# Transposed tiles by DMA in a two-layer transformer kernel: tokens and attention output leave TensorE and ScalarE

## The chip, the cores and the metric

One core of a Trainium2 chip runs the whole program. A core has five engines that each follow their own list of instructions in order: PE (TensorE, matrix products into the PSUM banks, with weight loads shown apart as PEld), DVE (VectorE), ACT (ScalarE), POOL (GpSimd, which has no access to PSUM) and SP (SyncE, which here only issues DMAs). They meet at semaphores. The metric is the device time of one execution in microseconds (us), the median of several.

## The reference

Two equal layers act on 2048 tokens of width 512. Each layer is an attention block with 32 heads of width 16 and a feed-forward block (FFN) of width 1792, both behind a layer norm and with a residual sum. Both layers use the same weights.

```python
x = A_x
x = x + _A_ref(_layernorm(x, axis=-1), A_wqkv, A_wo)
x = x + _B_ref(_layernorm(x, axis=-1), B_w_gate, B_w_up, B_w_down)
x = x + _A_ref(_layernorm(x, axis=-1), A_wqkv, A_wo)
x = x + _B_ref(_layernorm(x, axis=-1), B_w_gate, B_w_up, B_w_down)

# _A_ref: scores = q @ k.T * Dh ** -0.5; softmax over the keys; times v; heads joined; @ wo
# _B_ref: (gelu(x @ w_gate) * (x @ w_up)) @ w_down
```

## The kernel before

**Tiles.** X holds the tokens in float32, 16 tiles of 128 tokens on the partitions. A matrix product contracts over partitions, so each consumer needs its input transposed: XNT holds the normalised tokens with the model dimension on the partitions (four chunks of 128), ATTT the same for 128 tokens of attention output. KT holds the transposed keys, eight head groups (g, four heads each) by 2048 keys in four blocks of 512 (kb); a head has 32 rows there, 16 of keys and others that carry a bias of -1, so that the row maximum written beside the query is subtracted inside the product. QT holds up to eight units of queries in the same form.

**Two passes over the scores.** A unit is a block of 128 to 512 queries times one head group; there are 80. The first pass (line 1711) makes the scores with queries on the partitions and DVE takes the row maxima (line 1726, one or two banks at a time). The maxima are joined on POOL (lines 1071 to 1073), transposed in small blocks by DVE into MT, and SP moves them into QT (line 1115). The second pass (line 1581) makes the transposed scores with the maxima subtracted, ACT takes exponentials into SCR (line 1557), and PE multiplies them with the values (line 1605) into bank 7. A "fold" shifts work between the engines: PE makes the product of the queries with the difference of two key blocks (KD, line 1530), ACT takes its relu (line 1537), and DVE needs one combined step (line 1721) in place of the two blocks' maxima. `want_fold` decides by how far the first pass leads the second.

**The planner.** The order of every engine's instructions is written out when the program is built. Generators ("chains") yield what they need next: an engine with the tiles read and written, or a condition. The main loop of `_build` keeps an estimated clock for each engine, steps chains for DVE, POOL and ACT as soon as their operands are estimated ready, SP chains when the operands are due within 0.5 us and SP's clock within 0.8, and picks for PE between first pass, second pass and the rest by due times. Every DMA issue is estimated at 0.63 us of SP (`T_DMA`), and its end at 1.6 us later plus a given duration. When PE would stand still, the planner puts in products with a tile of zeros (line 1750). Every 16 steps of the first pass the next row of PLAN sets 21 constants, among them the lead at which copies go to DVE (LAGT), the thresholds for fillers, for folds and for how much other work PE takes between the passes.

**Where the tiles are transposed.** `ln_to_xnt` (line 874) normalises up to four tiles, by POOL alone (`ln_pool`), by DVE and POOL (`ln_head`), or in the head and the very last block by faster forms; the normalised tile goes to one of two buffers XN. Then `transpose_tile` (line 847) takes a bank, makes four PE transposes (line 855) and copies the bank to XNT with `evac`, on ACT (line 709) or DVE (line 707) by `pick`. Tags name the place: ("in", layer) ahead of the attention, ("mid", layer) ahead of the FFN. `outproj` does the same with ATT and two buffers ATTT, ahead of the product with WO. `ffn` takes a lock (`gel["on"]`) after its tiles are transposed in the plan; while it is held the second pass has no exponentials, since ACT has another function table loaded. In the head, six copies on ACT and two on POOL (line 564, `kt_fill`) fill KT with the bias rows before keys are moved in by SP (line 928).

```python
            if rd:
                for e, i in rd.items():
                    need((e, i))
```

These lines, in `_Sched.op`, turn a reader of a tile into a dependency of its next writer. A DMA group is a semaphore; a serial group counts its transfers one after another.

Of the kernel before, what the change touches and what calls it, by code (L numbers as in the profile page):

```python
# [21 lines left out]
    (0.2, 0.1, 0.55, 0.42, 0.3, -0.05, 1, 0, 30, 76, 8, 20, 0.3, 2.0, 0, 6, 1, 2, 9, 1, 0.0),  # L22
    (0.2, 0.1, 0.55, 0.42, 0.3, -0.05, 1, 0, 30, 76, 8, 20, 0.3, 2.0, 0, 6, 1, 2, 9, 1, 0.0),
    (0.1, 0.35, 0.65, 0.52, 0.2, -0.05, 1, 1, 102, 84, 13, 60, -0.1, 2.0, 0, 2, 1, 4, 5, 1, 0.0),
    (0.1, 0.15, 0.55, 0.32, 0.2, -0.05, 2, 1, 70, 84, -12, 40, 0.3, 2.0, 10, 2, 2, 2, 6, 1, 0.0),
    (0.3, 0.1, 0.55, 0.0, 0.0, -0.05, 2, 0, 14, 84, 8, 40, 0.3, 1.0, 0, 2, 2, 2, 5, 2, 0.0),
    (0.2, 0.1, 0.55, 0.42, 0.3, -0.05, 2, 0, 30, 84, 8, 60, 0.3, 2.0, -5, 2, 4, 3, 7, 1, -0.05),
    (0.2, 0.1, 0.65, 0.62, 0.3, -0.05, 1, 2, 30, 84, 8, 60, 0.3, 1.5, -5, 2, 4, 3, 9, 4, -0.05),
    (0.2, 0.1, 0.55, 0.62, 0.3, -0.05, 1, 2, 30, 84, 8, 60, 0.3, 2.0, -5, 2, 4, 3, 9, 1, -0.05),
    (0.2, 0.1, 0.55, 0.62, 0.3, -0.15, 1, 2, 30, 84, 8, 60, 0.3, 2.0, -5, 2, 4, 3, 9, 1, -0.05),  # L30
    (0.2, 0.1, 0.55, 0.62, 0.3, -0.15, 1, 2, 30, 84, 8, 50, 0.3, 2.0, -5, 2, 4, 2, 9, 1, -0.05),
    (0.2, 0.1, 0.55, 0.62, 0.3, -0.05, 1, 2, 30, 84, 8, 60, 0.3, 2.0, -5, 2, 4, 3, 9, 1, -0.05),
    (0.2, 0.1, 0.55, 0.62, 0.3, -0.1, 1, 2, 30, 116, 8, 60, 0.3, 2.0, -5, 2, 1, 3, 9, 1, -0.05),
    (0.4, 0.1, 0.65, 0.42, 0.3, -0.05, 3, 0, 5, 84, 8, 60, 0.3, 3.5, 20, 6, 2, 3, 3, 1, 0.2),
    (0.35, 0.15, 0.65, 0.12, 0.3, -0.05, 3, 0, 5, 84, 8, 60, 0.3, 1.0, 15, -6, 2, 3, 3, 1, 0.05),
    (0.2, 0.05, 0.55, 0.42, 0.3, -0.05, 2, 0, 30, 84, 8, 60, 0.3, 2.0, -5, 2, 4, 3, 7, 1, -0.05),
    (0.2, 0.05, 0.55, 0.42, 0.3, -0.05, 2, 0, 30, 84, 8, 60, 0.3, 2.0, -5, 2, 4, 3, 7, 1, -0.05),
    (0.2, 0.1, 0.55, 0.62, 0.3, -0.05, 1, 2, 30, 84, 8, 60, 0.3, 2.0, -5, 2, 4, 3, 9, 4, -0.05),
    (0.2, 0.1, 0.55, 0.52, 0.3, 0.0, 2, 0, 30, 84, 8, 60, 0.3, 2.0, -5, 2, 4, 3, 7, 1, -0.05),
    (0.15, 0.1, 0.55, 0.42, 0.0, -0.05, 3, 0, 70, 76, -2, 80, 0.7, 2.0, 15, 2, 2, 1, 7, 3, 0.2),  # L40
    (0.15, 0.1, 0.55, 0.32, 0.0, -0.05, 3, 0, 70, 76, -2, 80, 0.7, 2.0, 10, 2, 2, 1, 3, 3, 0.2),
    (0.3, 0.15, 0.55, 0.42, 0.2, 0.0, 2, 0, 38, 84, 8, 40, 0.3, 2.0, 0, -14, 2, 2, 5, 2, 0.0),
    (0.3, 0.15, 0.55, 0.42, 0.2, 0.0, 2, 0, 38, 84, 8, 40, 0.3, 2.0, 0, -14, 2, 2, 5, 2, 0.0),
    (0.1, 0.1, 0.55, 0.42, 0.0, -0.05, 2, 1, 70, 76, -2, 80, 0.7, 2.0, 10, 2, 2, 1, 7, 3, 0.2),
    (0.1, 0.1, 0.55, 0.42, 0.0, -0.05, 2, 1, 70, 76, -2, 80, 0.7, 2.0, 10, 2, 2, 1, 7, 3, 0.2),
    (0.1, 0.1, 0.65, 0.42, 0.0, -0.05, 2, 1, 70, 76, -2, 80, 0.7, 2.0, 10, 2, 2, 1, 7, 3, 0.2),
    (0.1, 0.1, 0.65, 0.42, 0.0, -0.05, 2, 1, 70, 76, -2, 80, 0.7, 2.0, 10, 2, 2, 1, 7, 3, 0.2),
    (0.1, 0.1, 0.55, 0.42, 0.0, -0.05, 2, 1, 70, 76, -2, 80, 0.7, 2.0, 10, 2, 2, 1, 7, 3, 0.2),
    (0.2, 0.05, 0.55, 0.42, 0.3, -0.05, 2, 0, 30, 84, 8, 60, 0.3, 2.0, -5, 2, 4, 3, 7, 1, -0.05),
    (0.2, 0.1, 0.55, 0.52, 0.3, -0.05, 1, 2, 30, 84, 3, 60, 0.3, 2.0, -5, -14, 4, 3, 9, 4, -0.05),  # L50
    (0.1, 0.3, 0.55, 0.42, 0.7, -0.1, 1, 1, 46, 84, 3, 80, 0.4, 2.5, -20, 10, 2, 1, 10, 1, 0.0),
    (0.15, 0.1, 0.55, 0.22, 0.0, -0.05, 2, 0, 62, 84, 8, 100, 0.3, 1.0, 0, 2, 2, 3, 7, 1, 0.0),
    (0.15, 0.1, 0.55, 0.42, 0.0, -0.05, 3, 0, 70, 76, -2, 80, 0.7, 2.0, 10, 2, 2, 1, 7, 3, 0.2),
    (0.15, 0.1, 0.55, 0.32, 0.0, -0.05, 3, 0, 70, 76, -2, 80, 0.7, 2.0, 10, 2, 2, 1, 3, 3, 0.2),
    (0.3, 0.1, 0.75, 0.22, 0.0, -0.05, 2, 0, 14, 84, 8, 40, 0.3, 1.0, -5, 2, 2, 2, 5, 2, 0.0),
    (0.15, 0.1, 0.55, 0.42, 0.0, -0.05, 3, 0, 70, 76, -2, 80, 0.7, 2.0, 10, 2, 2, 1, 7, 3, 0.2),
    (0.4, 0.1, 0.55, 0.42, 0.0, -0.05, 3, 0, 70, 76, -2, 80, 0.7, 2.0, 10, 2, 2, 1, 7, 3, 0.2),
# [1936 lines left out]
```

## Time and profile before

| | us |
|---|---|
| median of 3 runs | 2491.98 |
| lowest, highest | 2491.92, 2493.49 |
| the profiled execution, its own time | 2492.01 |
| its span in the trace | 2490.2 |
| PE, DVE, ACT, POOL busy in the span | 2416.1, 2397.1, 2350.7, 800.9 |

How to read the rows: a group's row names the line of the kernel, engine, operation, what is written and read, shapes and count; then the busy time of all and the mean in ns of one; then the idle time of the engine just before them and what ended it. Matmuls of PE overlap, so its sum of durations is no measure of its rate. A row of a view in order of time begins with the start and the length in us. In a view of waits stand the waiting instruction, the one that ended the wait, the total in us, the number and the longest. A DMA row of SP (SPq) gives the time that SP takes to issue it, and "landing" the time until the data have arrived.

### The profile page before, as it was taken

What the parts mean: (1) busy time and instruction counts of PE and PEld (TensorE: products, weight loads), DVE (VectorE), ACT (ScalarE), POOL (GpSimd) and SP (SyncE); (2) the same over time, 40 slices, a digit from 0 to 9 for tenths busy, and PEclk for the clock granted to TensorE, in tenths of its full rate; (3) what the DMA queues carried; (4) which work ended last, traced back from release to release, by engine and by line L of the source; (5) the groups of instructions that cost most, each with busy time, mean ns of one, the idle gap of its engine ahead of it and who ended that gap; (6) DMA issues with size and microseconds to landing.
All of it is one profiled execution on the core that took longest, in us unless ns stands there. A gap on an engine that the chain in (4) does not pass through costs nothing.

```text
span 2490.2 us, 69394 instructions
## 1 busy us (share of the span) xinstructions
PE 2416.1 (97%) x30236; PEld 1163.3 (47%) x30236; DVE 2397.1 (96%) x3163; ACT 2350.7 (94%) x3413; POOL 800.9 (32%) x1274
## 2 busy tenths in 40 slices
PE   8999999999999999999999999999999999999999
PEld 3444444354443445444534444434553445544656
DVE  8999999999999999999999999999999999998995
ACT  7999999999998999899989999999998999989987
POOL 4112125415533353241233141533113311343430
PEclk9999999999999999999999999999999999999999
DMA  3110000000000000000000000000000000000000
GB/s 96 46 57 6 4 9 4 2 2 6 4 3 3 4 2 6 4 4 15 11 10 2 10 13 6 2 6 8 4 4 6 5 8 3 2 4 9 8 3 11
DMA packets 28913, 25.68 MB, mean 10 GB/s; under 512 B 10944, under 2 KB 27584, under 8 KB 28608
## 3 DMA queue, kind: packets, MB, share of 16 engines
q1 hardware_dynamic: 28608, 21.24, 3.3%
q8 instruction: 237, 3.88, 0.7%
q14 instruction: 68, 0.56, 0.1%
HBM read 10.22 MB, written 2.10 MB: 5 GB/s over the span
## 4 chain that ended last, share of the span: by engine, by line
PE 47%; DVE 28%; ACT 23%; issue 1%; DMA 0%; SPq 0%; ACTq 0%
DVE PM L1726 26%; ACT SCR L1557 21%; PE PS L1711 15%; PE PS L692 13%; PE PS L1605 10%; PE PS L1581 4%; PE PS L1750 4%; DVE SCR L1721 1%; ACT SCR L1537 1%; PE PS L855 1%; PE PS L1530 0%; ACT AO L1192 0%; ACT XNT L709 0%; ACT SG L709 0%; ACT ATTT L709 0%
## 5 line engine op out<-in xcount | busy, mean ns | idle before, releaser
L1726 DVE TENSOR_REDUCE PM<-PS 128x2 f32<-128x1024 f32 (+1 forms) x2521 | 2212.5, 938 | 52.1 <-PE PS L1581 26.8
L1557 ACT ACTIVATE SCR<-PS 128x1024 bf16<-128x1024 f32 (+1 forms) x2687 | 2015.6, 859 | 43.3 <-PE PS L1581 28.6
L1711 PE MATMUL PS<-KT,QT 32*128 32x512 bf16 x3912 | 1019.1, 384 | 42.1 <-DVE PM L1726 26.1
L1581 PE MATMUL PS<-QT,KT 32*128 32x512 bf16 (+2 forms) x5120 | 926.1, 340 | 2.4 <-ACT SCR L1557 1.7
L1605 PE MATMUL PS<-VP,SCR 128*128 128x51 bf16 (+1 forms) x16384 | 803.3, 187 | 10.8 <-ACT SCR L1557 7.1
L1605 PEld LDWEIGHTS PS<-VP,SCR 128*128 128x128 bf16 x16384 | 572.8, 96 | 476.2 <-issue 398.5
L1711 PEld LDWEIGHTS PS<-KT,QT 32*128 32x128 bf16 x3912 | 244.1, 91 | 530.9 <-DVE PM L1726 297.2
L1750 PE MATMUL PS<-WV,ZER 128*128 128x240 bf16 x2252 | 412.4, 266 | 4.6 <-ACT SCR L1557 3.5
L1174 POOL TENSOR_TENSOR RL<-ACCS,CM 128x16 f32<-128x16 f32 (+2 forms) x71 | 182.5, 2571 | 441.4 <-ACT ACCS L1164 440.8
L1581 PEld LDWEIGHTS PS<-QT,KT 32*128 32x128 bf16 x5120 | 250.4, 91 | 67.4 <-ACT SCR L1557 38.0
L1750 PEld LDWEIGHTS PS<-WV,ZER 128*128 128x128 bf16 x2252 | 170.3, 96 | 59.4 <-issue 43.6
L1292 POOL TENSOR_TENSOR HT<-HT,AO 128x512 bf16<-128x512 bf16 x98 | 113.8, 1163 | 186.8 <-ACT AO L1290 186.7
L1071 POOL TENSOR_TENSOR PM<-PM 128x16 f32<-128x16 f32 (+3 forms) x142 | 32.6, 230 | 427.4 <-DVE PM L1726 411.7
L1329 POOL TENSOR_TENSOR KD<-KT 128x512 bf16<-128x512 bf16 x80 | 92.3, 1154 | 183.8 <-PE PS L1530 170.1
L692 PE MATMUL PS<-XNT,WU 128*128 128x512 bf16 (+2 forms) x504 | 132.3, 357 | 0.3
L692 PE MATMUL PS<-WD,HT 128*128 128x512 bf16 x448 | 129.7, 381 | 0.0
L1721 DVE CUSTOM_DVE_ANT_0 SCR<-PS,SCR 128x512 bf16<-128x512 f32 x184 | 118.7, 686 | 2.6 <-PE PS L1711 0.7
L1537 ACT ACTIVATE SCR<-PS 128x1024 bf16<-128x1024 f32 (+1 forms) x123 | 102.9, 836 | 18.6 <-PE PS L1530 18.3
L692 PE MATMUL PS<-XNT,WG 128*128 128x512 bf16 (+2 forms) x504 | 119.5, 358 | 0.5 <-ACT HT L1274 0.4
L1194 POOL TENSOR_TENSOR X<-X,AO 128x512 f32<-128x512 f32 x47 | 59.5, 1267 | 185.7 <-ACT AO L1192 185.6
L1274 ACT ACTIVATE HT<-PS 128x512 bf16<-128x512 f32 (+2 forms) x126 | 68.4, 550 | 38.9 <-PE PS L692 38.5
L692 PEld LDWEIGHTS PS<-XNT,WG 128*128 128x128 bf16 x504 | 37.5, 97 | 55.1 <-issue 30.1
(117 smaller groups left out, 1098.5 us busy)
## 6 DMA issues: line engine op xcount, KB each, us to landing
KT<-SG SPq DMA_DIRECT2D x64, 64.0 KB
QT<-MT SPq DMA_DIRECT2D x244, 1.0 KB
QT<-SG SPq DMA_DIRECT2D x56, 64.0 KB
out_dram<-AO SPq DMA_DIRECT2D x16, 128.0 KB, 1.7
WG<-in_B_w_gate_dram SPq DMA_DIRECT2D x4, 448.0 KB, 4.7
WU<-in_B_w_up_dram SPq DMA_DIRECT2D x4, 448.0 KB, 4.6
WD<-in_B_w_down_dram SPq DMA_DIRECT2D x4, 384.0 KB, 4.6
QT<-MT SPq DMA_DIRECT2D x68, 0.2 KB
```

The costliest lines, as they stand in the source:

```text
L692: ins = e.matmul(out_ap, lhsT=l, rhs=r_, start=(i == 0), stop=(i == n - 1))
L1174: emit("pool", lambda e: e.tensor_tensor(RL[:, s, 0:4 * nq], lsum, AP(CM1, 0, [[1, 128], [0, 4 * nq]]), op=ALU.pow), r=[("ACCS", s), ("CM1 ...
L1292: emit("pool", lambda e, ft=ft, o=o: e.tensor_tensor(HT[:, ft, c0:c0 + n], HT[:, ft, c0:c0 + n], AO[:, o, 0:n], op=ALU.mult), r=[("AO", o) ...
L1329: emit("pool", lambda e: e.tensor_tensor(KD[:, s, :], KT[:, g, ka * 512:(ka + 1) * 512], KT[:, g, kb * 512:(kb + 1) * 512], op=ALU.subtrac ...
L1537: emit("act", lambda e: e.activation(PT[:, s0:s0 + cnt, :], PS[:, bk:bk + cnt, :], ACTF.Relu), r=bks, w=[("PT", s0 + d) for d in range(cnt ...
L1557: emit("act", lambda e: e.activation(dst, src, ACTF.Exp, scale=DH ** -0.5), r=[BK[bk + i] for i in range(cnt)], w=[("PT", i) for i in slot ...
L1581: ins = e.matmul(bank(bk)[:, i * n:(i + 1) * n], lhsT=KT[32 * j:32 * j + 32, g, kt * 128:(kt + 1) * 128], rhs=QT[32 * j:32 * j + 32, s, 0: ...
L1605: ins = e.matmul(acc, lhsT=PT[:, slot, i * n + qt * 128:i * n + (qt + 1) * 128], rhs=AP(VP, (kt * H + 4 * g + j) * 17, [[NTT * H * 17, 128 ...
L1711: ins = e.matmul(bank(b), lhsT=QT[32 * j:32 * j + 32, s, qt * 128:(qt + 1) * 128], rhs=KT[32 * j:32 * j + 32, g, kb * 512:(kb + 1) * 512], ...
L1721: emit("dve", lambda e, i=i, b=b, sl=sl: e.tensor_tensor_reduce(PT[:, sl, :], bank(b), PT[:, sl, :], 1.0, -3.0e38, ALU.add, ALU.max, po[:, ...
L1726: emit("dve", lambda e: e.tensor_reduce(po, PS[:, bs[0]:bs[0] + cnt, :], axis=AX.X, op=ALU.max), r=bks, w=[("PM", sm) + h[1:] for h in hs] ...
L1750: return e.matmul(PS[:, b, NACC:512], lhsT=ZER[:, :], rhs=WV[:, 0, 0:512 - NACC], start=(b != 7), stop=(b != 7), skip_group_check=True)
```

## The change

Six things are different.

1. `dma_tile` makes a transposed tile with four transposing DMAs from SP, one for each chunk of 128 columns, each under one of four new serial groups. It takes the place of `transpose_tile` in `ln_to_xnt` and `outproj`, except in the head (("in", 0)), for the last tiles of the sequence ahead of the first layer's FFN and the second layer's attention, for the first layer's last attention block, and for the last block of all.
2. A DMA of a serial group waits for the group's previous DMA.
3. Two K bias fills stay in ACT's head (NFE=2). Four more come in halves of 1024 columns once all key blocks of group 0 are recorded (`fills_act`). The key projection of a pair of groups waits in the plan for its fills.
4. `ln_pool` also takes the second group of four tiles ahead of the last FFN (LM1=0).
5. All but a few of PLAN's 118 rows have other constants.
6. New defaults: NFE=2, NFA=6, LM1=0, DTX=2, DTA=2, T_TP=1.5.

```diff
 PLAN = [
-    (0.2, 0.1, 0.55, 0.42, 0.3, -0.05, 1, 0, 30, 76, 8, 20, 0.3, 2.0, 0, 6, 1, 2, 9, 1, 0.0),
...
+    (0.4, 0.1, 0.65, 0.32, 0.3, -0.05, 3, 0, 5, 84, 8, 60, 0.3, 3.5, 20, 6, 2, 3, 3, 1, 0.2),
+    (0.15, 0.1, 0.75, 0.42, 0.0, 0.0, 2, 2, 70, 76, -2, 80, 0.7, 2.0, 10, 2, 2, 1, 7, 3, 0.1),
...
+        if grp is not None and self.groups[grp] and o.idx:
+            need((grp, o.idx - 1))
...
+        tp_groups = ["tx0", "tx1", "ty0", "ty1"] if DTX or DTA else []
+        for g in tp_groups:
+            sch.add_dma_group(g, serial=True)
...
-        def kt_fill(g, eng):
+        filled = set()
+
+        def kt_fill(g, eng, b0=0, b1=NKB):
...
-                r=[("HT", 0)], w=[("KT", g, b) for b in range(NKB)], dur=1.8 if eng == "act" else 2.95)
-
-        N_FILL = 6
-        for g in range(N_FILL):
+                r=[("HT", 0)], w=[("KT", g, b) for b in range(b0, b1)], dur=0.05 + 0.438 * (b1 - b0) if eng == "act" else 0.74 * (b1 - b0))
+            if b1 == NKB:
+                filled.add(g)
+
+        N_FILL = NFA
+        for g in range(NFE):
             kt_fill(g, "act")
...
+        def fills_act():
+            yield ("cond", lambda: kt_rec.get((0, NKB - 1)) == 0)
+            for g in range(NFE, N_FILL):
+                for b in range(0, NKB, 2):
+                    yield ("act", [("HT", 0)], [("KT", g, b), ("KT", g, b + 1)])
+                    kt_fill(g, "act", b, b + 2)
...
+        def dma_tile(src_fn, rkeys, dst_fn, wkeys, grp):
+            def fn(e):
+                return [e.dma_start_transpose(dst_fn(ck), src_fn(ck)) for ck in range(NCK)]
+
+            emit("sp", fn, r=list(rkeys), w=list(wkeys), grp=grp, nd=NCK, dur=T_TP)
...
-            by_pool = tag != ("in", 0) and not fast and tts[0] < (LNT - 4 if tag == ("mid", NL - 1) else LNT)
+            by_pool = tag != ("in", 0) and not fast and tts[0] < (LNT - 4 if tag == ("mid", NL - 1) and LM1 else LNT)
...
+                if DTX and tag != ("in", 0) and not fast and (DTX == 1 or tag not in (("mid", 0), ("in", 1)) or tts[-1] * 128 + 128 < S):
+                    yield ("sp", [("XN", i % 2)], [("XNT", tt)])
+                    dma_tile(lambda ck, i=i: XN[:, i % 2, ck * 128:(ck + 1) * 128], [("XN", i % 2)],
+                             lambda ck, tt=tt: XNT[:, ck, tt * 128:(tt + 1) * 128], [("XNT", tt)], "tx%d" % (i % 2))
+                    xnt_rec[tt] = tag
+                    at["tr"] = i
+                    continue
...
+            yield ("cond", lambda: 2 * c in filled and 2 * c + 1 in filled)
...
+            te = "sp" if DTA and not lastb and (DTA == 1 or la or t0 + n < S) else "pe"
...
+                if te == "sp":
+                    dma_tile(lambda ck: ATT[:, qt, ck * 128:(ck + 1) * 128], ak,
+                             lambda ck: ATTT[:, qt % 2, ck, :], [("ATTT", qt % 2)], "ty%d" % (qt % 2))
...
-            yield ("pe", ak, [("ATTT", 0)])
+            yield (te, ak, [("ATTT", 0)])
...
+        add(fills_act(), 0)
```

More of the change, by code (lines that the diff above doesn't have):

```diff
@@ L315, in _build @@
 def _build(nc, x_in, wqkv, wo, wg, wu, wd, out, layer_blocks=((512, 512, 512, 512), (512, 512, 512, 256, 128, 128)), ffn_groups=((512, 512, 512, 512), (512, 512, 512, 384, 128)),
[L316 removed]
+           n_ahead=6, n_pre=6, S1C=0.45, S2C=0.42, OV=0.3, PD=80, FDUE=20, LIM=-0.05, NT=1, AHD=2.0, DUEM=2, FDL2=0, OPD=12, URG=0.3, ft_tok=512, n_pt=8, n_qt=8, SPLIT=0.15, SPC=0.1, PVC=47, WARM=0.55, WARML=0.42, NPV=7, BOOST=0.0, LAG=62, LAGT=84, GP=2, SING=0, DUE=0, END=360, LAGE=10, FD=205, FDL=-10, QD=32, KD_=16, VD=20, FL=8, FMAX=6, NKD=2, FLOOK=2, FX=0.3, GF=1, NSPL=5, HSPL=0, TSPL=1, HNA=3, TNA=3, PB=1, OVF=0.0, FNP=1, NSG=3, LNT=8, HV=16, TW=0.95, HF=60, VS=14, SO=1.0, SF=1, SP=0, FAST=1, P2B=1, PIECE=2, GL=60, GLE=20, HARD=-1e9, VPARK=60, RUSH=1, XL=1000, NFE=2, NFA=6, LM1=0, DTX=2, DTA=2, T_TP=1.5):
     S = x_in.shape[1]
@@ L1205, in outproj @@
             nq = n // 128
+            te = "sp" if DTA and not lastb and (DTA == 1 or la or t0 + n < S) else "pe"
             def tr(qt):
-                transpose_tile(lambda ck: ATT[:, qt, ck * 128:(ck + 1) * 128], ak, ATTT[:, qt % 2, :, :],
-                               [("ATTT", qt % 2)])
+                if te == "sp":
+                    dma_tile(lambda ck: ATT[:, qt, ck * 128:(ck + 1) * 128], ak,
+                             lambda ck: ATTT[:, qt % 2, ck, :], [("ATTT", qt % 2)], "ty%d" % (qt % 2))
+                else:
+                    transpose_tile(lambda ck: ATT[:, qt, ck * 128:(ck + 1) * 128], ak, ATTT[:, qt % 2, :, :],
+                                   [("ATTT", qt % 2)])
                 if qt == nq - 1:
                     att_free["bi"] = bi
-            yield ("pe", ak, [("ATTT", 0)])
+            yield (te, ak, [("ATTT", 0)])
             tr(0)
@@ L1217, in outproj @@
                 if qt + 1 < nq:
-                    yield ("pe", ak, [("ATTT", 1 - s)])
+                    yield (te, ak, [("ATTT", 1 - s)])
                     tr(qt + 1)
```

5 lines of the change are left out of this document (2 added, 3 removed), and 233 rows, old and new, of the table PLAN.

## The prediction, made before the changed kernel ran

> **What bounds the kernel now.** I read first the busy shares and the chain of the page, then the groups kept apart by form, then the span cut into twenty equal windows.
>
> ```profile
> span 2490.2 us, 69394 instructions
> PE 2416.1 (97%) x30236; PEld 1163.3 (47%) x30236; DVE 2397.1 (96%) x3163; ACT 2350.7 (94%) x3413; POOL 800.9 (32%) x1274
> PE 47%; DVE 28%; ACT 23%; issue 1%; DMA 0%; SPq 0%; ACTq 0%
> L1750 PE MATMUL PS<-WV,ZER 128*128 128x240 bf16 x2252 | 412.4, 266 | 4.6 <-ACT SCR L1557 3.5
> ```
>
> PE shows the largest share, but 412.4 us of it are the zero-weight fillers of L1750, which the planner puts in when nothing else is due. The two engines without filler are DVE (row maxima of the scores) and ACT (exponentials and most copies out of PSUM). Together they work 2397.1 + 2350.7 = 4747.8 us of a possible 2 x 2490.2 = 4980.4, so 232.6 us idle, 116 each. The next rows show busy time in five windows of 124.5 us; the columns after the length are PE, PEld, DVE, ACT, POOL, then granted clock and DMA share.
>
> ```profile
> 0.00:124.50 124.50, 110.19 (x970) 46.47 (x971) 114.96 (x183) 101.25 (x148) 38.31 (x75) 1.00 0.25 71
> 373.50:498.00 124.50, 120.46 (x1345) 51.85 (x1341) 123.15 (x172) 117.16 (x163) 60.83 (x98) 1.00 0.01 3
> 498.00:622.50 124.50, 121.38 (x1609) 59.01 (x1607) 122.80 (x145) 122.08 (x183) 44.43 (x60) 1.00 0.02 4
> 996.00:1120.50 124.50, 122.09 (x1306) 51.95 (x1305) 118.40 (x143) 109.27 (x154) 44.36 (x62) 1.00 0.02 4
> 2365.50:2490.00 124.50, 120.28 (x1874) 73.81 (x1874) 94.75 (x154) 102.56 (x171) 23.46 (x61) 1.00 0.03 7
> ```
>
> In a plain stage (498 to 622.5) DVE and ACT are both at 98%: the stage ends when their joint work is done. In a stage with a gate phase ACT is short of work (7.3 us idle from 373.5, 15.2 from 996, where DVE is short of 6.1 too). Head and tail idle most: (9.5 + 23.2) / 2 = 16 us and (29.8 + 21.9) / 2 = 26 us per engine. So the price of an edit in the middle is half the DVE plus ACT work that it takes away, if the planner can trade between the two, plus new idle time.
>
> **The change, part by part.**
>
> Removed: 66 transposed tiles leave PE and ACT. By the conditions in the diff these are, of normalised tokens, 12 before the first FFN, 12 before the second attention and 15 before the second FFN (its last 128 tokens stay), and of attention output 12 and 15. Each was four PE transposes and one copy out of PSUM.
>
> ```profile
> L709 ACT ACTIVATE XNT<-PS 128x512 bf16<-128x512 bf16 x56 | 35.1, 636 | 3.2 <-PE PS L855 3.2
> L709 ACT ACTIVATE ATTT<-PS 128x512 bf16<-128x512 bf16 x32 | 20.5, 646 | 2.1 <-PE PS L855 2.1
> L707 DVE COPY XNT<-PS x4: 410/413/425, 33.8 to 2198.6; 128x512 bf16<-128x512 bf16 x4
> 22.64 0.40 PE L855 MATMUL PS<-IDN,XN 128*128 128x128 bf16 x4
> L789 DVE BATCH_NORM_STATS2 ST<-X 128x6 f32<-128x512 f32 x27 | 18.4, 683 | 0.0
> L791 DVE BATCH_NORM_AGGREGATE MV<-ST 128x2 f32<-128x6 f32 x27 | 4.9, 182 | 0.9
> ```
>
> Attention: 27 x 0.646 = 17.4 us of ACT. Normalised: past the head only 3 or 4 of these copies are on DVE, so 36 x 0.636 = 22.9 us of ACT and 3 x 0.413 = 1.2 of DVE. PE loses 66 x 0.40 = 26 us, which filler or earlier work takes up: worth nothing by itself. LM1=0 moves the norms of four more tiles from DVE to POOL: 4 x (0.683 + 0.182) = 3.5 us of DVE; POOL, 32% busy, covers it (without that cover it would cost the wait for one POOL norm). Together ACT loses 40.3 and DVE 4.7 us.
>
> How ACT's relief reaches DVE: when the second pass catches up, the planner makes folds, in which ACT takes a relu of a pair of banks and DVE then does two short steps for two double reductions.
>
> ```profile
> L1726 DVE TENSOR_REDUCE PM<-PS 128x2 f32<-128x1024 f32 x1207 | 1459.5, 1217 | 38.2 <-PE PS L1581 19.9 <-PE PS L1711 7.4 <-PE PS L1530 0.4
> L1537 ACT ACTIVATE SCR<-PS 128x1024 bf16<-128x1024 f32 x61 | 65.5, 1073 | 3.2 <-PE PS L1530 3.0
> L1721 DVE CUSTOM_DVE_ANT_0 SCR<-PS,SCR 128x512 bf16<-128x512 f32 x184 | 118.7, 686 | 2.6 <-PE PS L1711 0.7 <-PE PS L1581 0.4
> L1721 DVE DVE_READ_ACCUMULATOR2_ANT PM<- 128x1 f32 x184 | 15.3, 83 | 0.0
> ```
>
> A pair costs ACT 1.073 and saves DVE 2 x 1.217 - 2 x (0.686 + 0.083) = 0.90, an exchange of 0.84. With f us of ACT spent so, 40.3 - f = 4.7 + 0.84 f gives f = 19.3 and a gain of **21.0 us**. If no fold is added, DVE remains the bound and the gain is 4.7. I take 21.0, because the rule that makes folds looks only at how far the first pass leads.
>
> Added: 264 transposing DMAs, four to a tile, on SP. The trace has none, so bounds come from its other transfers.
>
> ```profile
> L1115 SPq DMA_DIRECT2D QT<-MT x344: 497/521/828, 66.8 to 2452.7; - x172
> L928 SPq DMA_DIRECT2D KT<-SG x64: 461/596/1837, 16.4 to 1401.5; - x64
> out_dram<-AO SPq DMA_DIRECT2D x16, 128.0 KB, 1.7
> q1 hardware_dynamic: 28608, 21.24, 3.3%
> SPq L1115 <- DVE MT L1075: 1317.7, 57, 42.1
> ```
>
> Low end: an issue of 0.521 and a landing of 1.7, so 4 x 0.521 + 1.7 = 3.8 us for a tile. A packet takes 0.033 x 16 x 2490.2 / 28608 = 46 ns of one engine, so if a tile goes as 512 rows of 256 B it moves in 512 x 0.046 / 16 = 1.5 us, under its issue time. High end of issue: 1.837 each, 7.3 us a tile and 9.0 to landing. If every element were a packet, one tile would take 188 us and the kernel over 12 ms; the diff calls a transposing instruction and no element-wise access pattern, so I give that under 1 in 100 and leave it out. I take the low end, nearest in kind (SBUF to SBUF, SP, four in a row), which needs 264 x 0.521 = 138 us of SP in all. SP waits 1317.7 us for the row maxima alone, so it has room; but it is in order. Behind a transposing DMA that waits for its source or issues late stand the query loads and the QT<-MT transfers, and for these wait the exponentials of that unit and the first pass six units on. The planner orders SP by its own estimate of 0.63 per issue, 0.11 more than the row, so I cost this at nothing.
>
> The Trainium skill speaks against the low end: "VectorE: DVE Perf Modes", section "The three transpose paths", gives 1309 ns for a 128x128 tile by DMA against 390 on TensorE. No run so far shows the DMA figure, while the row above has four TensorE transposes in 0.40 us, so a burst is far cheaper there than four times the page's figure. By the page four DMAs would need an estimated 5.2 us, 3.1 more than four issues by the row, and the sum would go to the slower rival below.
>
> New idle time: ffn() takes the gelu lock (no exponentials) as soon as its last tile is issued in the plan, not when it has landed.
>
> ```profile
> L801 POOL TENSOR_SCALAR XN<-X,LNS x27: 767/771/786, 964.2 to 2401.9; 128x512 bf16<-128x512 f32 x27
> 419.32 0.64 ACT L709 ACTIVATE XNT<-PS 128x512 bf16<-128x512 bf16 x1
> 420.27 0.67 ACT L1537 ACTIVATE SCR<-PS 128x512 bf16<-128x512 f32 x1
> 422.29 1.28 ACT L1274 ACT_TABLE_LOAD   x1
> ACT HT L1274 <- PE PS L692: 38.5, 66, 1.2
> ```
>
> Now the last copy (419.32) is 3 us ahead of the gate phase (422.29). With a tile of 3.8 us in place of 0.40 + 0.64 the lock is about 2.8 us longer, in 3 groups of the first layer and 4 of the second: 20 us of ACT if nothing fills it, 10 us of span. The fold at 420.27 shows that relus are allowed there; I take half, **5 us** lost. Within a group a tile comes every 0.77 us from POOL but XN has two buffers, so the norms of four tiles last about 15 us; that lies ahead of work due much later, beside the maxima and exponentials.
>
> Moved: four of six K bias fills leave ACT's head and come back as eight half pieces.
>
> ```profile
> L564 ACT COPY KT<-HT 128x2048 bf16<-128x2048 bf16 x6 | 10.9, 1894 | 0.0
> 4.91 10.90 ACT L564 COPY KT<-HT 128x2048 bf16<-128x2048 bf16 x6
> 15.71 0.62 ACT L827 ACTIVATE X<-HT 128x512 f32<-128x512 bf16 x1
> HT<-in_A_x_dram SPq DMA_DIRECT2D x2, 512.0 KB, 8.7
> 3.88 2.34 SPq L501 DMA_DIRECT2D HT<-in_A_x_dram  x2
> 39.25 0.60 ACT L709 ACTIVATE VP<-PS 128x512 bf16<-128x512 f32 x1 [1.11 <-PE PS L692]
> ```
>
> ACT's next work (15.71) needs tokens that land near 3.88 + 8.7 = 12.6, so it can begin up to 3.1 us sooner. The pieces, 0.95 us each, fall in gaps like the 1.11 us ones about 39 us; without them 7.6 us of ACT, 3.8 of span. Between 0 and 3.1 I take **2 us** gained.
>
> The other edits. Serial groups wait for their own previous DMA: the other groups' slots were reused only after that had landed, cost nothing (an issue each, were it not so). The constants change only order and balance: from no gain to a fourth of the 74 us per engine that idle between head and tail (116 - 16 - 26), so 18 either way; I take 0, since no row says which sign.
>
> Sum against the profiled execution: 2490.2 - 21.0 + 5 - 2 = 2472.2 span. That execution took 2492.01 us, 1.8 outside the span, and the median shown is 2491.98, so **2474**.
>
> **The rivals.**
>
> Slower: the transposes come later than planned and PE, in order, stands before the product that reads them. That is 27 attention tiles and 10 groups of normalised tokens, 37 waits. DVE and ACT hold about one double instruction, 1.2 us; beyond this a late tile of x us idles both for x - 1.2. It eats the whole gain (18) from x = 1.7. At the high end of issue, 4 x (1.837 - 0.63) = 4.8, it would cost 133; at half of that, x = 2.4, 44 - 18 = +26: **2518**. For it: no transposing DMA is in the trace and the longest issue is 1.837. Against it: 344 QT<-MT issues have a median of 0.521. The skill's 1309 ns, as an estimate, is x = 4 x (1.309 - 0.63) = 2.7, just above this rival. Chance 0.20.
>
> No gain: the lock hides nothing and SP is busy with a QT<-MT set when the last tile is ready, 2.1 us more: 7 x (2.8 + 2.1) = 34 us of ACT, and only part of the folds is added. Half of 34 is 17; with 4 us less from folds, 21 of the 21 + 2 us are lost: **2490**. For it the 38.5 us that ACT already waits for gate products; against it the fold at 420.27. Chance 0.10.
>
> More gain: the constants also take a fourth of the middle idle, 18 us: **2456**. For it DVE's 118.40 and ACT's 109.27 in the window from 996; against it 98% in the plain stages. Chance 0.17.
>
> **How the numbers follow.** The forecast has 0.53; its own range is 2463 (no lock cost and the head's full gain, 2468, with 5 from the constants) to 2485 (no folds added: 4.7 + 2, no lock cost on DVE). About 5 us, 0.2%, can be told from no change. Faster by more: 0.53 + 0.17 + 0.01 = 0.71; same 0.08 and slower 0.01 from the no-gain case; with the slower rival 0.21. The range 2452 to 2505 leaves out most of the slower rival and the far end of the constants.
>
> **What would show it.** Right: transposing DMAs of some 0.5 us issue, about 27 fewer ATTT and 36 fewer XNT copies on ACT, more relus of L1537 and fewer double reductions, DVE and ACT both down by about 20 us with the idle time as before. Wrong: PE or PEld waiting for DMA at products of XNT or ATTT by more than some 30 us in all, SP issues near 1.3 us or more, ACT idle ahead of each table load, or a granted clock under 1.00 where PE stood.

## The result, and the profile after

The kernel is slower: 2587.6 us, the median of 4 runs (2583.3 to 2593.63), against 2491.95 for the kernel before (2491.92 to 2493.49). The ratio is 1.0384, with an interval from 1.0371 to 1.0397. The forecast was 2474, and the range ended at 2505. The profiled execution shown below took 2588.97 us. (PLAN has 132 rows; the 118 named above are those that the diff replaces.)

| us | before | after |
|---|---|---|
| span | 2490.2 | 2587.2 |
| ACT busy, idle | 2350.7, 139.5 | 2339.0, 248.2 |
| DVE busy, idle | 2397.1, 93.1 | 2388.2, 199.0 |

Both engines that bound the kernel before have less to do, and each is idle for more than 100 us longer. The page of the changed kernel has its span, its busy shares, the granted clock in 40 slices, the chain of work that ended last, and the landing of the new DMAs:

```profile
span 2587.2 us, 69128 instructions
PE 2437.6 (94%) x29839; PEld 1161.0 (45%) x30039; DVE 2388.2 (92%) x3169; ACT 2339.0 (90%) x3416; POOL 807.7 (31%) x1311
...
PEclk8999998999889999999999999999999999989999
...
PE 45%; ACT 24%; DVE 19%; SPq 6%; POOL 2%; DMA 2%; issue 2%; POOLq 0%; ACTq 0%
...
XNT<-XN SPq DMA_TRANSPOSE x156, 2.3
...
ATTT<-ATT SPq DMA_TRANSPOSE x108, 2.3
```

SP's queue stood in the chain with 0%. It now has 6%, some 155 us of the 2587.2, and DMAs have 2% where they had 0%. The landing, 2.3 us, is 0.6 above the row that the forecast used; the larger miss is in the issues. The view of one tile's instructions gives, behind the count, the shortest, median and longest duration in ns, then the first and last start:

```profile
L879 SPq DMA_TRANSPOSE ATTT<-ATT x108: 1094/1233/2327, 356.6 to 2488.6; - x108
```

```profile
L879 SPq DMA_TRANSPOSE XNT<-XN x156: 1095/1232/2598, 412.7 to 2506.9; - x156
```

SP needs 1.23 us for each, where a plain QT<-MT issue needs 0.521. Four take 4.93 us; the planner books 4 x 0.63 = 2.52 and puts every other engine's work in order by that. In the waits one sees who stands when the tiles are late (engine, what it was to write, line, what it waited for; total, number, longest). First the kernel after, then the same places before, where line 692 is the later 708, 1581 is 1618, 1530 is 1567, and 1557 and 1537 are 1594 and 1574:

```profile
ACT SCR L1594 <- PE PS L1618: 66.6, 141, 5.3
ACT SCR L1574 <- PE PS L1567: 61.1, 77, 9.1
ACT HT L1310 <- PE PS L708: 57.1, 73, 11.4
...
POOL XN L795 <- DMA XNT<-XN: 30.0, 10, 6.0
PE PS L708 <- DMA XNT<-XN: 29.5, 6, 8.2
...
PE PS L708 <- DMA ATTT<-ATT: 15.8, 10, 5.0
...
PEld PS L708 <- DMA ATTT<-ATT: 4.7, 3, 2.5
```

```profile
ACT SCR L1557 <- PE PS L1581: 28.6, 100, 1.2
...
ACT SCR L1537 <- PE PS L1530: 18.3, 44, 1.0
```

PE waits 29.5 + 15.8 + 4.7 = 50.0 us for the new DMAs, in 19 waits, up to 8.2 at a time. For the QT<-MT transfers, which can stand behind these on SP, it waits only 2.2 us, so it is the tiles themselves that come too late. ACT waits 38.0 us more for scores, 42.8 more for the products of folds and 18.6 more for gate products (57.1 against 38.5). Not all of this is lateness: with one DMA for a tile, below, ACT still waits 18.5 us more for folds than before.

The first layer's first gate phase shows how. Three views of the kernel after, in order of time (start, length, engine, what, number; in brackets the idle time ahead and what ended it): SP, ACT, PE.

```profile
412.66 10.02 SPq L879 DMA_TRANSPOSE XNT<-XN  x8
422.73 2.21 SPq L1145 DMA_DIRECT2D QT<-MT  x4
...
426.16 10.47 SPq L879 DMA_TRANSPOSE XNT<-XN  x8
```

```profile
426.53 1.09 ACT L1594 ACTIVATE SCR<-PS 128x512 bf16<-128x512 f32 x2 [3.26 <-PE PS L1618]
435.09 0.60 ACT L1574 ACTIVATE SCR<-PS 128x512 bf16<-128x512 f32 x1 [7.48 <-PE PS L1567]
439.49 0.60 ACT L1574 ACTIVATE SCR<-PS 128x512 bf16<-128x512 f32 x1 [3.80 <-PE PS L1567]
440.10 1.28 ACT L1310 ACT_TABLE_LOAD   x1
```

```profile
428.23 0.38 PE L1748 MATMUL PS<-KT,QT 32*128 32x512 bf16 x1
...
430.00 0.61 PE L1748 MATMUL PS<-KT,QT 32*128 32x512 bf16 x2
...
431.79 1.58 PE L1787 MATMUL PS<-WV,ZER 128*128 128x240 bf16 x7
...
438.24 0.63 PE L708 MATMUL PS<-XNT,WG 128*128 128x512 bf16 x1 [2.76 <-DMA XNT<-XN]
```

Four tiles of four DMAs hold SP for 20.5 us in all (booked: 10.1), and four QT<-MT transfers go between them. The last tile's issues end at 436.63, and the first gate product follows at 438.24. The gelu lock is taken in the plan when those issues are planned, so ACT's list has no exponential between 427.6 and the table load at 440.10: it stands 7.48 and 3.80 us ahead of two folds. From 430.00 at the latest PE is slow, as the windows show (length; busy of PE, PEld, DVE, ACT and POOL; granted clock; DMA share; GB/s):

```profile
424.00:430.00 6.00, 4.97 (x36) 2.34 (x35) 5.41 (x12) 1.09 (x2) 1.16 (x8) 0.89 0.13 26
430.00:442.00 12.00, 9.24 (x35) 2.74 (x36) 6.01 (x7) 3.08 (x5) 0.00 (x0) 0.50 0.11 23
```

Over 12 us the granted clock is 0.50, DVE works 6.0 and ACT 3.1. The clock falls within the six microseconds from 424 (mean 0.89), in which PE was busy for only 4.97, so ahead of the wait at 438.24. The whole execution has a mean clock of 0.976, against 1.000 before.

What was meant to be removed did go. Groups of the kernel after (busy and mean ns, then idle time before them):

```profile
L1574 ACT ACTIVATE SCR<-PS 128x512 bf16<-128x512 f32 (+1 forms) x150 | 115.0, 767 | 63.1 <-PE PS L1567 61.1
...
L1758 DVE CUSTOM_DVE_ANT_0 SCR<-PS,SCR 128x512 bf16<-128x512 f32 x204 | 131.7, 687 | 21.1 <-PE PS L1748 17.1
```

```profile
L725 ACT ACTIVATE XNT<-PS 128x512 bf16<-128x512 bf16 x23 | 13.8, 611 | 7.0 <-PE PS L871 6.8
...
L725 ACT ACTIVATE ATTT<-PS 128x512 bf16<-128x512 bf16 x5 | 3.1, 612 | 1.9 <-PE PS L871 1.8
```

ATTT has 27 copies fewer on ACT (32 to 5) and XNT 33 fewer (56 to 23; 36 were expected). The fold's relus stood at this before, with 184 combined steps of DVE:

```profile
L1537 ACT ACTIVATE SCR<-PS 128x1024 bf16<-128x1024 f32 (+1 forms) x123 | 102.9, 836 | 18.6 <-PE PS L1530 18.3
```

### The profile page after: what moved, and what is told of

The parts are those of the page before. It is cut to its first block, busy times and chain, and to the rows that moved or that the text cites. A ratio compares the mean times of both kernels' runs of the same rounds, so it can differ in the third digit from the quotient of the medians.

```text
span 2587.2 us, 69128 instructions
## 1 busy us (share of the span) xinstructions
PE 2437.6 (94%) x29839; PEld 1161.0 (45%) x30039; DVE 2388.2 (92%) x3169; ACT 2339.0 (90%) x3416; POOL 807.7 (31%) x1311
## 4 chain that ended last, share of the span: by engine, by line
PE 45%; ACT 24%; DVE 19%; SPq 6%; POOL 2%; DMA 2%; issue 2%; POOLq 0%; ACTq 0%
ACT SCR L1594 22%; DVE PM L1763 18%; PE PS L1748 14%; PE PS L708 13%; PE PS L1642 10%; SPq L879 5%; PE PS L1618 4%; PE PS L1787 3%; DMA ATTT<-ATT 1%; DVE SCR L1758 1%; ACT SCR L1574 1%; DMA XNT<-XN 1%; POOL RL L1204 1%; PE PS L1567 0%; DMA HT<-in_A_x_dram 0%
## 5 line engine op out<-in xcount | busy, mean ns | idle before, releaser
L1763 DVE TENSOR_REDUCE PM<-PS 128x1 f32<-128x512 f32 (+1 forms) x2498 | 2194.1, 939 | 122.6 <-PE PS L1618 51.0
L1594 ACT ACTIVATE SCR<-PS 128x1024 bf16<-128x1024 f32 (+1 forms) x2722 | 2007.4, 854 | 82.9 <-PE PS L1618 66.6
L1748 PE MATMUL PS<-KT,QT 32*128 32x512 bf16 x3892 | 1026.4, 391 | 47.5 <-DVE PM L1763 29.5
L1787 PE MATMUL PS<-WV,ZER 128*128 128x240 bf16 x2319 | 428.5, 269 | 6.9 <-ACT SCR L1594 5.3
L1328 POOL TENSOR_TENSOR HT<-HT,AO 128x512 bf16<-128x512 bf16 x92 | 106.6, 1161 | 212.7 <-ACT AO L1326 212.6
L1574 ACT ACTIVATE SCR<-PS 128x512 bf16<-128x512 f32 (+1 forms) x150 | 115.0, 767 | 63.1 <-PE PS L1567 61.1
L708 PE MATMUL PS<-XNT,WG 128*128 128x512 bf16 (+2 forms) x489 | 129.7, 386 | 31.0 <-DMA XNT<-XN 29.5
L1758 DVE CUSTOM_DVE_ANT_0 SCR<-PS,SCR 128x512 bf16<-128x512 f32 x204 | 131.7, 687 | 21.1 <-PE PS L1748 17.1
L708 PE MATMUL PS<-XNT,WU 128*128 128x512 bf16 (+2 forms) x451 | 120.0, 354 | 5.8 <-issue 2.7
L708 PE MATMUL PS<-WD,HT 128*128 128x512 bf16 x388 | 115.8, 380 | 6.1 <-issue 4.4
L1310 ACT ACTIVATE HT<-PS 128x512 bf16<-128x512 f32 (+2 forms) x126 | 68.4, 549 | 57.8 <-PE PS L708 57.1
```

Source lines behind the costliest of these rows:

```text
L708: ins = e.matmul(out_ap, lhsT=l, rhs=r_, start=(i == 0), stop=(i == n - 1))
L1328: emit("pool", lambda e, ft=ft, o=o: e.tensor_tensor(HT[:, ft, c0:c0 + n], HT[:, ft, c0:c0 + n], AO[:, o, 0:n], op=ALU.mult), r=[("AO", o) ...
L1574: emit("act", lambda e: e.activation(PT[:, s0:s0 + cnt, :], PS[:, bk:bk + cnt, :], ACTF.Relu), r=bks, w=[("PT", s0 + d) for d in range(cnt ...
L1594: emit("act", lambda e: e.activation(dst, src, ACTF.Exp, scale=DH ** -0.5), r=[BK[bk + i] for i in range(cnt)], w=[("PT", i) for i in slot ...
L1748: ins = e.matmul(bank(b), lhsT=QT[32 * j:32 * j + 32, s, qt * 128:(qt + 1) * 128], rhs=KT[32 * j:32 * j + 32, g, kb * 512:(kb + 1) * 512], ...
L1758: emit("dve", lambda e, i=i, b=b, sl=sl: e.tensor_tensor_reduce(PT[:, sl, :], bank(b), PT[:, sl, :], 1.0, -3.0e38, ALU.add, ALU.max, po[:, ...
```

## The experiments

Each was timed beside the kernel before, which had a median between 2492.04 and 2492.21 in these comparisons. In the first three sections the booking stays at 2.52 us of SP, so that the planner makes the same order of work as in the changed kernel; only the time that SP really needs differs. The traces bear this out: DVE, ACT and POOL have the same instructions in the same sequence in all of them. For this the planner's function takes a booking of its own:

```diff
-        def emit(eng, fn, r=(), w=(), dur=0.1, grp=None, nd=1):
+        def emit(eng, fn, r=(), w=(), dur=0.1, grp=None, nd=1, iss=None):
-                clk[eng] = start + T_DMA * nd
+                clk[eng] = start + (T_DMA * nd if iss is None else iss)
```

### One DMA for a whole tile, same order

```diff
-                return [e.dma_start_transpose(dst_fn(ck), src_fn(ck)) for ck in range(NCK)]
+                return e.dma_start_transpose(dst_fn(slice(0, NCK)), src_fn(slice(0, NCK)))
-            emit("sp", fn, r=list(rkeys), w=list(wkeys), grp=grp, nd=NCK, dur=T_TP)
+            emit("sp", fn, r=list(rkeys), w=list(wkeys), grp=grp, nd=1, dur=T_TP, iss=2.52)
-                    dma_tile(lambda ck, i=i: XN[:, i % 2, ck * 128:(ck + 1) * 128], [("XN", i % 2)],
+                    dma_tile(lambda ck, i=i: XN[:, i % 2, :], [("XN", i % 2)],
-                    dma_tile(lambda ck: ATT[:, qt, ck * 128:(ck + 1) * 128], ak,
+                    dma_tile(lambda ck: ATT[:, qt, :], ak,
```

> One transposing DMA of 128x512 for each tile in place of four of 128x128; the planner books the same 2.52 us of SP for it, so every engine's order is as in the changed kernel. Theory 'late tiles, by the cost of an issue': one issue costs far less than the 4.9 us of four (between 1.2 and 2.5), and the time falls to 2490 to 2530. Rival 'the cost is in the transposing itself': the one issue or its landing takes 4 to 5 us, and the time stays within 10 us of 2588.

Measured: 2492.78 us (2491.68 to 2501.68), ratio 1.0009 (1.0 to 1.0019). The issues of this kernel, in the views by tile:

```profile
L879 SPq DMA_TRANSPOSE XNT<-XN x39: 1188/1213/2367, 404.3 to 2406.3; - x39
```

```profile
L879 SPq DMA_TRANSPOSE ATTT<-ATT x27: 1189/1220/2088, 349.7 to 2386.8; - x27
```

A DMA of 128x512 holds SP for 1.213 us, as long as one of 128x128 does. So the price is one for each instruction, whatever its size here, and a quarter of the instructions takes away 94.8 us, with no other change to the order. PE's waits for XNT and ATTT are gone. The rival, that one issue or its landing would take 4 to 5 us, is out: the landing is 2.4 us.

It doesn't get below the kernel before, though. Its page; then ACT, first on the first tokens in the head and then ahead of the same gate phase; then ACT's wait ahead of folds:

```profile
span 2490.3 us, 69130 instructions
PE 2417.1 (97%) x30039; PEld 1153.3 (46%) x30039; DVE 2381.7 (96%) x3169; ACT 2333.6 (94%) x3416; POOL 807.6 (32%) x1311
...
XNT<-XN SPq DMA_TRANSPOSE x39, 2.4
```

```profile
12.52 0.63 ACT L843 ACTIVATE X<-HT 128x512 f32<-128x512 bf16 x1 [2.94 <-DMA HT<-in_A_x_dram]
...
417.09 1.09 ACT L1594 ACTIVATE SCR<-PS 128x512 bf16<-128x512 f32 x2 [2.16 <-PE PS L1618]
424.13 0.60 ACT L1574 ACTIVATE SCR<-PS 128x512 bf16<-128x512 f32 x1 [5.96 <-PE PS L1567]
...
425.82 1.28 ACT L1310 ACT_TABLE_LOAD   x1
```

```profile
ACT SCR L1574 <- PE PS L1567: 36.8, 72, 6.0
```

ACT works 17.1 us less than before and DVE 15.4 less, and the span is the same: all of the relief has become idle time. Of ACT's waits the one ahead of folds grew, by 18.5 us (36.8 from 18.3), in stretches up to 6.0 us like the 5.96 here, inside the lock. DVE is idle for 108.6 us, 15.5 more than before, and of its waits none grew by more than 6 us; where its relief went isn't shown.

### Two DMAs for a tile, same order

The function takes the number of DMAs (np_), 2 at both places.

```diff
-                return [e.dma_start_transpose(dst_fn(ck), src_fn(ck)) for ck in range(NCK)]
+                return [e.dma_start_transpose(dst_fn(slice(c, c + NCK // np_)), src_fn(c, c + NCK // np_)) for c in range(0, NCK, NCK // np_)]
-            emit("sp", fn, r=list(rkeys), w=list(wkeys), grp=grp, nd=NCK, dur=T_TP)
+            emit("sp", fn, r=list(rkeys), w=list(wkeys), grp=grp, nd=np_, dur=T_TP, iss=2.52)
```

> Order of every engine as in the changed kernel, each tile by two transposing DMAs of 128x256 in place of four of 128x128. Theory 'an issue costs 1.2 us whatever its size, and only what exceeds the booked 2.52 hurts': two issues are 2.45 us, under the booking, so the time is 2490 to 2500, as with one DMA. Rival 'each issue costs its share, booked or not': a third of the way from one to four issues, 2493 + 95 / 3 = about 2525.

Measured: 2495.77 us (2492.27 to 2500.87), ratio 1.0017 (1.0007 to 1.0027). An issue of 128x256:

```profile
L879 SPq DMA_TRANSPOSE ATTT<-ATT x54: 1167/1247/2302, 351.0 to 2389.3; - x54
```

Two take 2.49 us, which just fits the booking of 2.52, and the time is within 0.2% of the kernel before, as the theory had it. Four take 4.93 and it is 92 us longer. Inside the booking there is next to no loss, beyond it there is; at which excess it begins, no run between the two shows.

### One DMA at one place only, same order

Here one place keeps four DMAs, and the other has one: first one for normalised tokens (attention output by four), then one for attention output (tokens by four). The edit is the last one with other numbers:

```diff
-[("XNT", tt)], "tx%d" % (i % 2), 2)
+[("XNT", tt)], "tx%d" % (i % 2), 1)
-[("ATTT", qt % 2)], "ty%d" % (qt % 2), 2)
+[("ATTT", qt % 2)], "ty%d" % (qt % 2), 4)
```

and the two numbers exchanged.

> Order as in the changed kernel; normalised tokens by one DMA for a tile, attention output by four. Theory 'the loss lies where late tiles meet the gelu lock', that is at the normalised tokens: most of the 95 us go, 2500 to 2525. Rival 'attention output is read at once by each product with WO, 27 waits against 10': the time stays at 2550 to 2580.

> Order as in the changed kernel; attention output by one DMA for a tile, normalised tokens by four. Theory 'gelu lock and normalised tokens': still 2560 to 2585. Rival 'attention output': 2500 to 2530. If both halves matter alike, both this and the twin run come near 2540.

Measured: 2534.73 us (2528.69 to 2539.26), ratio 1.0166 (1.0147 to 1.0185), with four at the attention output; 2546.7 (2540.6 to 2550.94), ratio 1.0217 (1.0197 to 1.0236), with four at the tokens. PE's waits in the one and in the other:

```profile
PE PS L708 <- DMA ATTT<-ATT: 14.9, 10, 4.2
```

```profile
PE PS L708 <- DMA XNT<-XN: 29.7, 7, 9.6
```

And ACT's waits, in the same order:

```profile
ACT SCR L1594 <- PE PS L1618: 68.0, 140, 4.9
```

```profile
ACT SCR L1574 <- PE PS L1567: 62.1, 77, 8.7
ACT HT L1310 <- PE PS L708: 60.7, 74, 13.2
```

Against 2492.78 with one DMA everywhere, attention output by four costs 42 us and tokens by four 54. Together that is 96, and the changed kernel stands 95 above the same point: the two add up, and nothing else in the order is needed for the loss. So both named theories were wrong, each of which put most of it at one place; the remark that both runs come near 2540 if the halves matter alike was right. The two places also reach ACT by different ways. With one DMA everywhere ACT waits 35.0 us for scores, 36.8 for folds and 35.5 for gate products. Late attention output raises the first alone (to 68.0), late tokens the other two (to 62.1 and 60.7).

### Four DMAs, booked at what they take

The default of T_TP goes from 1.5 to -0.5, so that a tile's end is estimated 1.1 us behind its last issue, and

```diff
-            emit("sp", fn, r=list(rkeys), w=list(wkeys), grp=grp, nd=NCK, dur=T_TP)
+            emit("sp", fn, r=list(rkeys), w=list(wkeys), grp=grp, nd=NCK, dur=T_TP, iss=4.93)
```

> The four DMAs of a tile as in the changed kernel, but the planner books what the trace shows: 4.93 us of SP for the four and an end 1.1 us after the last issue. Theory 'late tiles, by booking': PE's waits for DMA and the drop of the clock go away and the time falls to 2500 or less. Rival 'gelu lock': the lock is still held while SP issues, ACT idles ahead of each gate phase as before, and the time stays above 2550.

Measured: 2575.51 us (2570.39 to 2579.52), ratio 1.0332 (1.0315 to 1.0349), granted clock 0.995. PE's waits:

```profile
PE PS L708 <- DMA XNT<-XN: 7.8, 4, 3.7
...
PE PS L708 <- DMA ATTT<-ATT: 1.7, 4, 0.7
```

PE now hardly waits, 9.5 us in place of 45.3 in these two rows, and yet only 12 us came back. The waits and the clock that the theory spoke of did recover, but the time stayed where the rival had it. ACT waits 34.0 us for folds there (61.1 in the changed kernel), but 83.3 for gate products and 81.4 for scores. So the wait for late tiles isn't the only way to lose time here. A booking that is right gives another order, for which the constants of PLAN weren't made. The next two show how much that alone can do.

### No transposing DMA at all, and a nudge to the kernel before

First, all tiles of the changed kernel by PE and a copy again, everything else kept:

```diff
-DTX=2, DTA=2
+DTX=0, DTA=0
```

> The changed kernel with its new constants, fills and POOL norm, but every tile transposed by PE and copied by ACT or DVE again (DTX=0, DTA=0). Theory 'late tiles': the whole 96 us come from the transposing DMAs, so this lands at 2480 to 2510, granted clock 1.00 again. Rival 'constants': the new constants or the moved fills cost most of it, so this stays above 2550.

Measured: 2577.66 us (2570.35 to 2587.15), ratio 1.0345 (1.0319 to 1.037), though no such DMA is left. Two windows of this kernel:

```profile
1992.00:2116.50 124.50, 121.80 (x1219) 48.52 (x1219) 81.78 (x110) 113.13 (x193) 29.05 (x47) 0.99 0.02 7
2116.50:2241.00 124.50, 113.35 (x1433) 60.29 (x1432) 121.26 (x143) 86.50 (x103) 21.70 (x35) 0.99 0.02 3
```

DVE does 81.8 of 124.5 us in the first and ACT 86.5 in the second. It looks as if first and second pass had fallen out of step, so that one engine has little to do while the other catches up. My theory had it that undoing the DMAs would take most of the loss away; it doesn't, because this order loses about as much without them.

Then the kernel before, with one booking moved by 0.01 us and no instruction added or removed by hand:

```diff
-T_DMA = 0.63
+T_DMA = 0.62
```

> The kernel before with one number of the planner changed: it books 0.62 us of SP for a DMA issue in place of 0.63. No operation and no cost on the chip is changed, only the order that the planner writes. Theory 'the constants fit one order only' (why PE tiles under the new constants took 2578 and honest bookings 2576): 2510 to 2580. Rival 'constants are robust, and the new ones are simply bad': within 10 us of 2492.

Measured: 2552.48 us (2550.61 to 2554.88), ratio 1.0242 (1.0227 to 1.0258). A change of booking too small to matter on the chip costs 60 us. The three new orders with old constants tried so far stand 60 to 86 us above the kernel before: the constants of PLAN seem to fit only the order that they were made for. That is why a kernel with an altered plan can't be set against one with a fitted plan to price an edit, and why the comparisons above that keep the order carry the verdict.

### The lock later

The lock is taken only when the last tile is estimated to have landed.

```diff
-yield ("cond", lambda: gel["on"] is None)
+yield ("cond", lambda: gel["on"] is None and est(xk) <= clk["pe"] + 0.5)
```

> The changed kernel, but the gelu lock is taken only when the planner expects the last normalised tile within 0.5 us; bookings as in the changed kernel. Theory 'gelu lock': the 5 to 15 us that ACT idles ahead of each of 7 gate phases shrink, and the time falls by 30 to 60 us, to 2530 to 2560. Rival 'booking alone': the tiles still come later than booked, PE stands the same, and the time stays within 10 us of 2588.

Measured: 2588.66 us (2585.07 to 2606.07), ratio 1.04 (1.0365 to 1.0436), the same as the changed kernel. The time is the rival's. ACT's waits ahead of folds and gate products did shrink (33.1 us from 61.1, and 46.4 from 57.1), but its wait for scores grew to 99.6 from 66.6. This run decides little: the estimate it goes by is the short booking, and the order is new with old constants.

### One DMA, with constants of its own

Three kernels with the constants of PLAN fitted anew: one DMA for a tile with the late lock, the same with the lock as the change has it, and as a control the kernel before.

> One transposing DMA for a tile, the gelu lock taken only when the last tile is expected within 0.5 us, and the constants fitted anew to the order that results. Theory 'the relief of ACT is real, and was lost to the lock and to four issues': ACT's and DVE's idle time ahead of the gate phases shrinks and the time is 2475 to 2485, faster than both kernels. Rival 'the relief cannot be used, because DVE and ACT idle elsewhere instead': 2488 to 2496, as with one DMA alone.

> As the run with the late lock, but the lock is taken as in the changed kernel; one DMA for a tile, constants fitted anew. Theory 'the lock took the gain': about 2490, no better than one DMA alone, and some 8 us above the run with the late lock. Rival 'fitting the constants is the gain': as fast as the run with the late lock, within 3 us.

> The kernel before, tiles by PE, with only its constants fitted anew in the same way: the control for the two runs above. Theory 'the gain is from DMA tiles and the late lock': 2488 to 2492. Rival 'fitting the constants is the gain': 2475 to 2485.

| | median us | lowest, highest | ratio to before |
|---|---|---|---|
| one DMA, late lock | 2483.64 | 2482.34, 2492.47 | 0.9974 (0.9965 to 0.9984) |
| one DMA, lock as in the change | 2490.41 | 2489.02, 2497.98 | 1.0002 (0.9993 to 1.001) |
| before, constants alone | 2490.95 | 2490.89, 2491.66 | 0.9995 (0.9986 to 1.0003) |

The first is faster than both kernels; its interval stays below 1. New constants alone bring nothing that can be told, and neither do one DMA and new constants with the early lock. ACT in the fastest, ahead of the same gate phase, and its wait ahead of folds:

```profile
418.14 6.08 ACT L1594 ACTIVATE SCR<-PS 128x512 bf16<-128x512 f32 x11 [0.34 <-PE PS L1618]
424.27 0.60 ACT L1574 ACTIVATE SCR<-PS 128x512 bf16<-128x512 f32 x1
...
426.12 1.28 ACT L1310 ACT_TABLE_LOAD   x1
```

```profile
ACT SCR L1574 <- PE PS L1567: 18.9, 42, 1.0
```

Eleven exponentials now stand where ACT was idle for 5.96 us. The wait ahead of folds is back at 18.9 us, from 35.4 with the early lock and constants of its own. The step from the early to the late lock, 6.8 us, holds two sets of constants too, so its size isn't the lock's alone.

The trace of the kernel with the early lock is of an execution of 2497.34 us, 6.9 above the median. Its granted clock is 0.51 from 20 to 41 us, in the head, where the kernel before and the one with the late lock have 1.00. The waits ahead of folds lie behind that, so the 35.4 us don't hang on it; what lowers the clock there, no run isolates.

## Why the prediction was wrong, step by step

**The step that failed is the price of the added DMAs**: "I take the low end, nearest in kind (SBUF to SBUF, SP, four in a row)", 0.521 us an issue, and with it "so I cost this at nothing" for SP. An issue took 1.23 us, nearly in the middle (1.18) between the ends 0.521 and 1.837. The nearest row in place and route was not the nearest in operation, since no transposing DMA was in the trace. SP had the room (it waits 1317.7 us for the row maxima), but room over the whole span said nothing about the moment: SP's list, and all that is ordered around it, was written with 2.52 us a tile. The runs that hold the order fixed put all but 1 us of the loss there: 2587.6 us with 4.93 us of issues for a tile, 2495.77 with 2.49 and 2492.78 with 1.21.

The Trainium skill, "VectorE: DVE Perf Modes", section "The three transpose paths", had 1309 ns for a 128x128 tile by DMA. It doesn't say whether that is the issue or the time to landing; of the two the issue agrees within 6% (1.233 us here), while the landing took 2.3. That a 128x512 takes 1.213 to issue shows the price to be one of the instruction here.

**The slower rival was the right mechanism, and undersized.** Its lateness, x = 2.4 us a tile, is what came: 4 x (1.233 - 0.63) = 2.41. Its price was not: 37 waits at x - 1.2 gave 44 us, and 95 came (2587.6 against 2492.78), though PE stood for these DMAs only 19 times. It counts 27 x 1.2 = 32 for attention output, where the runs show 42, and 10 x 1.2 = 12 for the tokens, where they show 54. For the tokens it took one lateness for a group, while four tiles follow each other on SP and the delays add: 4 x 2.41 = 9.6 us at the last one, and 10 x (9.6 - 1.2) = 84 as an upper end. PE's direct waits are 50 us of the loss. The mean clock of 0.976 is what an estimated 124 us at 0.50 would give (2587.2 x 0.024 / 0.50), against none in the middle with one DMA (mean 1.000). How the rest of the loss divides between this low clock and the work piled up behind a wait, no run separates.

**The lock** was costed at 5 us: seven groups of 2.8 us are 20 of ACT and 10 of the span, and half of that was taken. In the changed kernel ACT is without exponentials from 427.6 to 440.1 at one place, 12.5 us. With one DMA and the same order it is from 418.2 to 425.8 there, 7.6 us; the other 4.9 come with the late tiles. But even so, with issues inside the booking, ACT loses 18.5 us more ahead of folds (36.8 against 18.3), close to the 20 that the step named before halving it twice. The cover it counted on, the fold at 420.27, is one relu in a stretch of 6 us. So with its transposes in time the change lands at 2492.8 (2490.4 with constants of its own), near the rival "No gain" at 2490. Of that rival's conditions the lock came, for ACT; the busy SP didn't at this place, where the third tile's norm ends at 415.85 and its issue begins at 416.00. That the lock is all of it isn't shown, since DVE's added idle time has no such wait.

**The relief was sized about right.** 27 and 33 copies left ACT. Folds went from 184 to 204 combined steps and ACT's relus from 102.9 to 115.0 us, 12.1 of the 19.3 that the exchange had worked out. With one DMA a tile ACT works 17.1 us less and DVE 15.4, where 21 each had been worked out. The half-sum of 16 us is what was there to win; one DMA, the late lock and its constants won 8.6 of it together (2492.21 to 2483.64).

**The head** began as worked out: with one DMA a tile ACT starts on the first tokens at 12.52 in place of 15.71, and the estimate was near 12.6. A gain of its own at the end isn't shown by any run.

**The constants** were given a bound of 18 us either way and a value of 0. The bound was far too small: 60 us for a nudge of the booking, 86 for the changed kernel's constants without its DMAs. For the order that the change plans they are good (2492.8 with one DMA), so they aren't the cause of its loss; they are why no part that alters the order can be undone alone.

**What was to show it wrong** did: PE waiting 50.0 us for XNT and ATTT (limit some 30), issues at 1.23, ACT idle ahead of table loads, and a clock of 0.50 where PE stood.

## What to carry to other kernels

Where an instruction isn't in the trace, a row of the same route is no price for it: work the sum out over the whole range between the bounds before taking one end at nothing (here the middle, 1.18 us, was close, which one case doesn't make a rule), and ask how late the last of several in a row comes, not the first. In a kernel whose order is planned with estimates, compare an engine's real issue time with what the plan books at that place; if it is over, use fewer and larger instructions before anything else. Test such an edit with the order held fixed, because a plan with fitted constants can lose more by a new order (60 to 86 us here) than the edit is worth.

## What the runs showed of the hardware

An issue of a transposing DMA held SP for 1.233 us at 128x128, 1.247 at 128x256 and 1.213 at 128x512 (medians), so four times the data cost the same there. Plain transfers from MT to QT on the same queue took 0.521. The landing hardly grew either, 2.3 us for 128x128 and 2.4 for 128x512 tokens. In the gate phase with late tiles the granted clock stood at 0.50 for 12 us, though fillers ran in it (431.79); it was back at 0.93 from 442 to 444, some 4 us after the first product with the late tile. In the kernel with one DMA it isn't lower there at all (1.00 from 405 to 435). What drops it no run isolates.
